# Block means of the second batch by narrow products and transposes, and the last store from another queue

## The chip, the cores and the metric

The kernel runs on one core of a Trainium2 chip. The metric is the device time of one execution in microseconds, the median of several runs; lower is better. TensorE (PE in the profile, PEld for its weight loads) multiplies, VectorE (DVE), ScalarE (ACT) and GpSimd (POOL) do the rest, and SyncE (SP) issues the transfers.

## The reference

Attention over 2 batches, 8 heads, 768 positions and 64 channels, followed by two feed-forward layers on the 1536 tokens:

```
k_sum = k.reshape(B, H, nb, 32, D).max(axis=3)      # nb = 24 blocks of 32 positions
v_sum = v.reshape(B, H, nb, 32, D).mean(axis=3)
scores_l = scale * (q @ k^T), kept where |i - j| < 16
scores_s = scale * (q @ k_sum^T) + log(32)
a = softmax(concat(scores_l, scores_s))
attn = a @ concat(v, v_sum)
x = attn as [1536, 512]
x = ((x @ w_a) * (x @ w_b)) @ w_out                  # width 1536
h = x @ w_in;  out = (h - tanh(h)) @ w_out2          # width 2048
```

What the change touches is `v_sum` of the second batch: 24 means for each of 8 heads and 64 channels, 24 x 512 numbers from 768 x 512.

## The kernel before

The 1536 tokens are three blocks of 512. The first layer runs over blocks and over 12 slices of its width: for each slice a position "a" (x @ w_a, bank "pa"), a position "b" (x @ w_b, bank "pb") and a position "o" (the product added into four banks "acc"). So a block has 36 positions, numbered j = 0, 1, 2 and so on over all blocks. The second layer follows with positions "h" and "o2". Each large product is made of three fp32r products of high and low halves, so that a projection of one slice is 12 matmuls of 512 columns (`proj`, line 374).

The attention of the first eight units of 64 queries is done ahead in an order written out by hand. The other 16 units are planned into the positions of the first layer: `plan(j, fn)` runs a step ahead of position j. A unit goes through T1 (transposes of q, line 269), T2 (scores, line 295, fp32, and softmax), T3 (transposes, line 331) and T4 (product with v, line 344, eight products into two halves of the partitions). In the same positions the weights are decoded (lines 154 to 165) and split in high and low halves (lines 184 and 185) on ScalarE, VectorE and GpSimd.

The order of the instructions on an engine is in part written out and in part found. From position 0 to 71 only SP's order is the program's; on the other engines a planner at build time chooses the order by its own costs and by priorities (the steps T1, T2, T3, T4, W and prep_k get a higher one). From position 72 on all engines follow the program's order. Each engine then works through its list in that order, and waits when an operand isn't ready.

The second batch's means are one step, `mean_v`, planned at position VM + NC + 4 = 13. Before it six transfers load v of that batch in chunks of 128 positions with all eight heads (`load_vch`), two chunks each in the tiles x20a and x20b and two in buffers of the tag "w", which has 36 buffers. The step multiplies each chunk with a slice of a constant, `mavg` [128, 44], that holds 1/32 where a position belongs to a block, and adds all six into one bank "pt" of 24 x 512. ScalarE copies it to a buffer of "w", and `load_vm` copies that by transfers behind the 96 rows of v in the tiles of units 12 to 14. The bank "pt" is also used by T1 and T3 and by half of prep_k.

The results of the last block are four banks of 128 rows. ScalarE copies the first and the third, VectorE the second and the fourth, and SP issues a store of 256 KB behind each copy (line 477).

Of the kernel before, what the change touches and what calls it, by code (L numbers as in the profile page):

```python
# [15 lines left out]
AF = mybir.ActivationFunctionType  # L16
# [23 lines left out]
def band_attention_moe_kernel(ctx: ExitStack, tc: tile.TileContext, q, k, v, w_a, w_b, w_out, w_in, w_out2, out):  # L40
    nc = tc.nc
    mm = nc.tensor.matmul
# [4 lines left out]
    NB = S // BLK  # L47
    NP = H // 2
    KC = DM // 128
    F1 = w_a.shape[1] // 128  # L50
    F2 = w_in.shape[1] // 128
    TB = 512
    NBLK = NT // TB
    NC = S // 128
# [8 lines left out]
    def st(shape, tag, bufs=1, dt=F32):  # L63
        return sb.tile(shape, dt, tag=tag, bufs=bufs, name=tag)

    def pt(tag, shape=(128, 512)):
        return ps.tile(list(shape), F32, tag=tag, name=tag)


    ident = st([128, 128], "ident")  # L70
# [3 lines left out]
    mavg = st([128, 2 * NB - 4], "mavg")  # L74
# [134 lines left out]
    def where(u):  # L209
        b, w = divmod(u, S // 64)  # L210
        return b, w, min(max(w * 64 - WIN, 0), S - KW)
# [18 lines left out]
    vch = {}  # L230
# [4 lines left out]


    def mean_v(tag):
        pp = pt(tag)[0:NB]
        for c in range(NC):
            mm(  # L240
                pp, mavg[:, NB - 4 - 4 * c : 2 * NB - 4 - 4 * c], vch.pop(c).rearrange("p h d -> p (h d)"),
                start=(c == 0), stop=(c == NC - 1),
            )
        vmo[1] = st([NB, H, D], "w", 3 * F1)
        nc.scalar.activation(vmo[1].rearrange("n h d -> n (h d)"), pp, AF.Copy)

# [201 lines left out]
    def late_hi_lo():  # L448
        if late:
            hi_lo(*late.pop())  # L450

    def pos_o2(G, s):
        blk, f = divmod(G, F2)
        if G == N2 - 1:
            late_hi_lo()
        gh, gl = gs.pop(1000 + G)
        if f == 0:
            acc[10 + blk] = [pt(f"acc{d}") for d in range(4)]
        a = acc[10 + blk]
        for c in range(4):  # L460
            cs = slice(c * 128, (c + 1) * 128)
            for n, (g, i) in enumerate(((gh, 0), (gh, 1), (gl, 0))):
                mm(a[c], g[:, cs], s[:, i, :], start=(f == 0 and n == 0), stop=(f == F2 - 1 and n == 2))  # L463
        if f == F2 - 1:
            if blk < NBLK - 1:
                t = [st([128, 2, DM], f"x2{blk}{i}") for i in "ab"]
                o = [t[c // 2][:, c % 2, :] for c in range(4)]
            else:
                t = st([128, 4, DM], "kt")
                o = [t[:, c, :] for c in range(4)]  # L470
            for c in range(4):
                if c % 2:
                    nc.vector.tensor_copy(o[c], a[c])
                else:
                    nc.scalar.activation(o[c], a[c], AF.Copy)
                r0 = blk * TB + c * 128
                nc.sync.dma_start(out[r0 : r0 + 128, :], o[c])


    HALF, WARM, VM, PK, KS = 0, 3, 3, -3, 2  # L480
# [24 lines left out]
    for G in range(N2 + LAG):  # L505
        if G < N2:
            pos.append((pos_h, G, 3 * F1 + 2 * (G % F2)))
        if G == 0:
            pos.append((pos_o, groups[-1], 3 * F1 - 1))
        if G >= LAG:  # L510
            pos.append((pos_o2, G - LAG, 3 * F1 + 2 * ((G - LAG) % F2) + 1))
# [39 lines left out]
    for c in range(NC):  # L551
        plan(VM + c, lambda c=c: load_vch(c, vt2[c // 2][:, c % 2] if c < 4 else st([128, H, D], "w", 3 * F1)))
    plan(VM + NC + 4, mean_v, "pt")
    OFF = -2
    for n, u in enumerate(range(8, 24)):
        j = (n - 8) * 4 + begin[1] + OFF if n >= 8 else n * (begin[1] // 8) + OFF
        b, w, _ = where(u)
# [280 lines left out]
```

## Time and profile before

| what | us |
|---|---|
| median of 3 runs | 666.63 (666.58 to 667.04) |
| profiled execution, whole | 668.39 |
| its span, first to last instruction | 666.6 |
| TensorE busy | 645.6 (97%) |
| VectorE busy | 509.3 (76%) |
| ScalarE busy | 471.9 (71%) |

The runs are without the profiler; the profiled execution is one more. Busy shares are averages over the span and say nothing of single stages. TensorE's matmuls overlap: the duration of one is longer than its distance to the next, so a pitch is read from the time of many. The granted clock is a share of full speed, 2.4 GHz.

### The profile page before, as it was taken

The page shows a single profiled execution, that of the slowest core. Times are in us where ns is not written, and L with a number is a line of the kernel's source. Part 1 is how long each engine was busy: PE and PEld are TensorE (multiplying, and loading weights), DVE is VectorE, ACT ScalarE, POOL GpSimd, SP SyncE. Part 2 cuts the span into 40 slices and gives each one's busy share as a digit, 9 for nine tenths or more (in the row PEclk, how much of TensorE's full clock was granted, in tenths as well). Part 3 has the DMA queues.
Part 4 walks back from the last instruction along what each step waited for, and adds up shares of the span by engine and source line. Part 5 has one row for each costly group of instructions (what it writes and reads, how often), then busy time and mean ns, then how long its engine had stood idle before and what let it go on. Part 6 is the DMA issues. An engine that isn't in the chain of part 4 may idle for free.

```text
span 666.6 us, 9629 instructions
## 1 busy us (share of the span) xinstructions
PE 645.6 (97%) x3240; PEld 520.3 (78%) x3240; DVE 509.3 (76%) x1019; ACT 471.9 (71%) x1002; POOL 208.1 (31%) x223
## 2 busy tenths in 40 slices
PE   7869999999899999999999999999999999999997
PEld 5658776888688888888888888888888888888885
DVE  5899998999766678637877748777777777777775
ACT  3878888788776778645655548777777777777774
POOL 5771122122001111000111134454444454444441
PEclk8989999999999999999999999999999999999999
DMA  9996996464415435413444200000010000010001
GB/s 205 246 204 202 214 225 184 152 187 132 129 55 168 151 107 167 131 48 111 142 143 142 80 1 0 1 0 1 0 64 1 0 1 0 24 40 1 1 0 63
DMA packets 84781, 62.11 MB, mean 93 GB/s; under 512 B 51892, under 2 KB 75444, under 8 KB 84732
## 3 DMA queue, kind: packets, MB, share of 16 engines
q1 hardware_dynamic: 84732, 61.50, 33.3%
q8 instruction: 25, 0.41, 0.2%
q14 instruction: 24, 0.20, 0.1%
HBM read 54.00 MB, written 7.34 MB: 92 GB/s over the span
## 4 chain that ended last, share of the span: by engine, by line
PE 84%; DVE 7%; ACT 3%; DMA 3%; issue 1%; SPq 1%; POOL 0%; DVEq 0%; ACTq 0%
PE acc L463 20%; PE pa L374 18%; PE pb L374 17%; PE acc L402 13%; PE pt L374 5%; PE ps L374 5%; PE ps L295 2%; PE ps L344 1%; PE pt L331 1%; DVE w L164 1%; PE pt L240 1%; DVE w L165 1%; DMA x20a<-in_q_dram 1%; SPq L614 1%; DMA w<-in_k_dram 1%
## 5 line engine op out<-in xcount | busy, mean ns | idle before, releaser
L185 POOL TENSOR_TENSOR wsp<-w,wsp 128x512 fp32r<-128x512 f32 x97 | 127.4, 1332 | 143.8 <-ACT wsp L184 143.8
L184 ACT ACTIVATE wsp<-w 128x512 fp32r<-128x512 f32 x201 | 121.3, 622 | 19.8 <-PE acc L402 10.1
L185 DVE TENSOR_TENSOR wsp<-w,wsp 128x512 fp32r<-128x512 f32 x104 | 74.7, 719 | 41.7 <-ACT wsp L184 41.5
L179 POOL TENSOR_SCALAR w<-w 128x512 f32<-128x512 f32 x52 | 39.5, 763 | 192.8 <-ACT w L154 184.0
L402 PE MATMUL acc<-gh,wsp 128*128 128x512 f32 x288 | 98.1, 400 | 0.0
L374 PE MATMUL pa<-XA,wsp 128*128 128x512 f32 x336 | 84.9, 399 | 4.6 <-DVE XA L726 4.6
L374 PE MATMUL pb<-XA,wsp 128*128 128x512 f32 x336 | 83.8, 395 | 0.9 <-ACT wsp L768 0.5
L463 PE MATMUL acc<-wsp,gh 128*128 128x512 f32 x256 | 80.5, 396 | 0.0
L374 PEld LDWEIGHTS pa<-XA,wsp 128*128 128x128 f32 x336 | 64.0, 191 | 18.7 <-ACT x21a L155 4.7
L374 PEld LDWEIGHTS pb<-XA,wsp 128*128 128x128 f32 x336 | 62.4, 189 | 15.2 <-ACT wsp L768 1.0
L367 ACT ACTIVATE gh<-tg 128x512 fp32r<-128x512 f32 x68 | 42.3, 622 | 30.6 <-DVE tg L390 30.2
L374 PE MATMUL pa<-XB,wsp 128*128 128x512 f32 x240 | 62.0, 402 | 1.4 <-ACT XB L351 1.4
L402 PEld LDWEIGHTS acc<-gh,wsp 128*128 128x128 f32 x288 | 53.4, 188 | 11.8
L374 PE MATMUL pb<-XB,wsp 128*128 128x512 f32 x240 | 60.0, 394 | 0.0
L402 PE MATMUL acc<-gl,wsp 128*128 128x512 f32 x144 | 56.9, 398 | 0.1
L463 PEld LDWEIGHTS acc<-wsp,gh 128*128 128x128 f32 x256 | 48.2, 188 | 11.1
L368 DVE TENSOR_TENSOR gl<-tg,gh 128x512 fp32r<-128x512 f32 x68 | 47.0, 691 | 9.4 <-ACT gh L367 9.3
L374 PEld LDWEIGHTS pa<-XB,wsp 128*128 128x128 f32 x240 | 45.2, 192 | 11.1 <-ACT XB L351 1.6
L374 PEld LDWEIGHTS pb<-XB,wsp 128*128 128x128 f32 x240 | 44.6, 188 | 9.7
L463 PE MATMUL acc<-wsp,gl 128*128 128x512 f32 x128 | 50.4, 394 | 0.0
L463 PE MATMUL acc<-wsp,vw 128*128 128x512 f32 x192 | 46.5, 390 | 0.0
L463 PEld LDWEIGHTS acc<-wsp,vw 128*128 128x128 f32 x192 | 35.9, 188 | 8.1 <-DVE vw L368 0.4
(305 smaller groups left out, 1184.0 us busy)
## 6 DMA issues: line engine op xcount, KB each, us to landing
stage<-in_moe_w_out_dram SPq DMA_DIRECT2D x19, 512.0 KB, 3.4
stage<-in_moe_w_in_dram SPq DMA_DIRECT2D x16, 512.0 KB, 5.2
stage<-in_moe_w_a_dram SPq DMA_DIRECT2D x8, 512.0 KB, 4.5
w<-wsc SPq DMA_DIRECT2D x16, 256.0 KB, 3.5
vw<-in_v_dram SPq DMA_DIRECT2D x19, 192.0 KB, 3.0
stage<-in_moe_w_b_dram SPq DMA_DIRECT2D x7, 512.0 KB, 5.0
wsc<-x21a SPq DMA_DIRECT2D x8, 256.0 KB, 4.8
wsc<-x21b SPq DMA_DIRECT2D x8, 256.0 KB, 5.9
```

The costliest lines, as they stand in the source:

```text
L164: nc.vector.scalar_tensor_tensor(r, t[:, :, 1], -0x40000000, r, op0=ALU.bitwise_and, op1=ALU.bitwise_or)
L165: nc.vector.tensor_tensor(r, r, t[:, :, 0], op=ALU.add)
L179: nc.gpsimd.tensor_scalar(rf, rf, HI_HI, HI_LO, op0=ALU.min, op1=ALU.max)
L184: nc.scalar.activation(s[:, 0, :], r, AF.Copy)
L185: eng.tensor_tensor(s[:, 1, :], r, s[:, 0, :].bitcast(F32), op=ALU.subtract)
L240: mm(pp, mavg[:, NB - 4 - 4 * c : 2 * NB - 4 - 4 * c], vch.pop(c).rearrange("p h d -> p (h d)"), start=(c == 0), stop=(c == NC - 1),)
L295: mm(pp[:, p, 0:NK], qt[:, p, :], kw[:, p, :], start=True, stop=True)
L367: nc.scalar.activation(dst[0], src, AF.Copy)
L368: eng.tensor_tensor(dst[1], src, dst[0].bitcast(F32), op=ALU.subtract)
L374: mm(dst, w, xx, start=(kk == 0 and n == 0), stop=(kk == KC - 1 and n == 2))
L402: mm(acc[blk][d][:, c0:c1], w, t, start=(f == 0 and c0 == 0 and n == 0), stop=(f == F1 - 1 and n == 2))
L463: mm(a[c], g[:, cs], s[:, i, :], start=(f == 0 and n == 0), stop=(f == F2 - 1 and n == 2))
```

## The change

The means of the second batch are computed the other way round. Instead of six products with the constant as weights and 512 columns of v streamed, there are 24 products, one for each chunk and pair of heads, with 128 columns of v (two heads of 64) as weights and 4 columns of the constant streamed; each writes its own 4 columns of a bank as [128 channels of a pair, pair, block]. ScalarE copies these 128 x 96 numbers to a new buffer of "w". Four transposes turn them into 24 x 512 in "pt" again, and the copy to the second buffer is as it was. Nothing is added up over chunks any more, since a block lies in one chunk.

The last of the twelve stores of results (block 2, rows 384 to 511) is issued from ScalarE's queue, the others from SP's as they were.

```diff
     def mean_v(tag):
+        pp = pt(tag)[:, 0 : NP * NB].rearrange("x (p n) -> x p n", p=NP)
+        for c in range(NC):
+            t = vch.pop(c)
+            for p in range(NP):
+                mm(pp[:, p, 4 * c : 4 * c + 4], t[:, 2 * p : 2 * p + 2, :], mavg[:, NB - 4 : NB], start=True, stop=True)
+        vt = st([128, NP, NB], "w", 3 * F1)
+        nc.scalar.activation(vt, pp, AF.Copy)
         pp = pt(tag)[0:NB]
-        for c in range(NC):
-            mm(
-                pp, mavg[:, NB - 4 - 4 * c : 2 * NB - 4 - 4 * c], vch.pop(c).rearrange("p h d -> p (h d)"),
-                start=(c == 0), stop=(c == NC - 1),
-            )
+        for p in range(NP):
+            nc.tensor.transpose(pp[:, p * 128 : (p + 1) * 128], vt[:, p, :], ident)
         vmo[1] = st([NB, H, D], "w", 3 * F1)
         nc.scalar.activation(vmo[1].rearrange("n h d -> n (h d)"), pp, AF.Copy)
...
                 r0 = blk * TB + c * 128
-                nc.sync.dma_start(out[r0 : r0 + 128, :], o[c])
+                (nc.scalar if blk == NBLK - 1 and c == 3 else nc.sync).dma_start(out[r0 : r0 + 128, :], o[c])
```

## Rows read from the trace of the kernel before

**Rows 1.** The page, busy time of each engine and its share of the span.

```profile
PE 645.6 (97%) x3240; PEld 520.3 (78%) x3240; DVE 509.3 (76%) x1019; ACT 471.9 (71%) x1002; POOL 208.1 (31%) x223
```

**Rows 2.** Stretches: busy time of each engine, granted clock, DMA share, GB/s.

```profile
core 0: us, PE busy (x) PEld busy (x) DVE busy (x) ACT busy (x) POOL busy (x), PEclk, DMA share, GB/s
...
106.00:160.00 54.00, 54.00 (x309) 44.19 (x310) 50.20 (x113) 44.07 (x104) 12.67 (x16) 1.00 0.49 150
160.00:176.00 16.00, 15.89 (x88) 12.14 (x87) 14.47 (x35) 13.44 (x35) 2.25 (x3) 1.00 0.47 146
...
285.00:661.00 376.00, 376.00 (x1638) 307.11 (x1637) 275.42 (x421) 256.83 (x453) 139.32 (x113) 1.00 0.10 36
```

**Rows 3.** The chain of waits, 95 to 125 us: start, us, piece, instructions.

```profile
99.79 0.88 PE ps L295 x8
100.67 5.26 PE pt L240 x12
105.93 2.96 PE pb L374 x12
108.90 0.23 PE acc L402
109.13 0.61 PE ps L344 x16
...
119.29 0.44 PE pt L331 x4
119.72 0.89 PE ps L295 x8
```

**Rows 4.** VectorE's timeline behind the step; in brackets the wait and its releaser.

```profile
106.51 0.17 DVE L322 RECIPROCAL sm<-sm 128x4 f32<-128x4 f32 x1
108.93 0.69 DVE L390 TENSOR_TENSOR tg<-pb,ta 128x512 f32<-128x512 f32 x1 [2.26 <-PE pb L374]
```

**Rows 5.** The step of line 240: ns min/median/max, first and last start, shape.

```profile
L240 PEld LDWEIGHTS pt<-x20a,mavg x4: 99/102/103, 100.6 to 101.5; 128*24 128x24 f32 x4
L240 PE MATMUL pt<-x20a,mavg x4: 592/592/610, 100.6 to 101.9; 128*24 128x512 f32 x4
```

**Rows 6.** Groups of weight loads by shape: busy us, mean ns of one, idle before.

```profile
L295 PEld LDWEIGHTS ps<-kw,qbd 128*128 128x128 f32 x96 | 12.6, 195 | 1.4 <-DVE XB L352 0.9
...
L344 PEld LDWEIGHTS ps<-at,vw 120*64 120x64 f32 x256 | 8.8, 137 | 5.4 <-issue 3.4 <-DVE w L161 1.1 <-DVE sm L321 0.4
...
L240 PEld LDWEIGHTS pt<-x20b,mavg 128*24 128x24 f32 x4 | 0.4, 103 | 1.3 <-issue 1.3
```

**Rows 7.** ScalarE's timeline around the step's copy.

```profile
106.05 0.57 ACT L245 ACTIVATE w<-pt 24x512 f32<-24x512 f32 x1
106.53 0.65 ACT L154 ACTIVATE w<-x21b 128x512 f32<-128x512 f32 x1
107.08 1.20 ACT L154 ACTIVATE w<-stage 128x512 f32<-128x512 f32 x2
```

**Rows 8.** Groups on ScalarE, 85 to 180 us: busy us, mean ns.

```profile
L351 ACT ACTIVATE XB<-ps 128x256 fp32r<-128x256 f32 x7 | 2.6, 368 | 0.0
```

**Rows 9.** Timeline of weight loads behind the step.

```profile
109.06 0.55 PEld L344 LDWEIGHTS ps<-at,vw 120*64 120x64 f32 x16 [0.36 <-issue]
109.67 0.20 PEld L269 LDWEIGHTS pt<-ident,w 128*128 128x128 f32 x2
```

**Rows 10.** Stretches around two changes of the granted clock (columns as in rows 2).

```profile
39.30:43.58 4.28, 0.21 (x7) 0.07 (x3) 4.28 (x11) 3.81 (x8) 4.20 (x6) 1.00 0.45 133
43.58:50.41 6.83, 5.86 (x15) 4.21 (x16) 6.62 (x13) 3.45 (x7) 3.03 (x3) 0.50 1.16 217
...
176.70:180.11 3.41, 1.54 (x15) 0.97 (x12) 1.81 (x3) 1.59 (x4) 0.00 (x0) 1.00 0.66 131
180.11:183.53 3.42, 3.42 (x12) 2.84 (x12) 1.52 (x11) 1.62 (x8) 0.00 (x0) 0.50 0.97 303
```

**Rows 11.** All stores of results: issue on SP, ns, first and last start; landing.

```profile
L477 SPq DMA_DIRECT2D out_dram<-kt x4: 332/332/332, 661.3 to 663.5; - x4
...
DMA to landing us min/median/max: 2.0/2.0/2.5
```

**Rows 12.** Timeline of the last copies.

```profile
661.33 2.50 SPq L477 DMA_DIRECT2D out_dram<-kt  x4
...
662.10 0.60 ACT L475 ACTIVATE kt<-acc 128x512 f32<-128x512 f32 x1 [0.79 <-PE acc L463]
662.78 0.69 DVE L473 COPY kt<-acc 128x512 f32<-128x512 f32 x1 [0.68 <-PE acc L463]
```

**Rows 13.** TensorE's timeline at the second fall of the clock.

```profile
179.52 1.55 PE L295 MATMUL ps<-kw,qbd 128*128 128x120 f32 x8 [0.44 <-DVE XB L352]
```

**Rows 14.** What weight loads waited for, 106 to 176 us: total, times, longest.

```profile
PEld pt L331 <- ACT e L324: 0.9, 4, 0.4
PEld pb L374 <- ACT wsp L184: 0.8, 1, 0.8
```

## The prediction

> **What bounds the kernel now.** I read the page's busy times first: TensorE is busy for 97% of the span, VectorE for 76%, ScalarE for 71% [rows 1]. An average hides stages, so the next view is the table of stretches around the edit: between 106 and 160 us TensorE is busy for all of 54.00 us, between 160 and 176 for 15.89 of 16.00, and from 285 to 661 us without a gap [rows 2]. The chain of waits says the same in order of time: from 100 to 125 us each piece is a TensorE piece [rows 3]. VectorE is close behind (50.20 of 54.00 us), but right behind the step that is changed it is VectorE that waits for TensorE, 2.26 us at 108.93 us [rows 4]. So a microsecond that TensorE gains or loses in this step should reach the end nearly whole. The one larger rest of TensorE behind it, 176.70 to 180.11 us with 1.54 us of work [rows 10], is a dependency of the attention on block 1, which moves along with TensorE.
>
> **The products.** Today the step is six fp32 products that show as 12 weight loads of 24 columns and 12 matmuls of 512 columns [rows 5]; in the chain they take 5.26 us, 0.44 us each [rows 3]. In the change each of 24 products has 128 columns of v as weights and streams 4 columns. The products of scores (line 295) show how one splits: four of them are 8 loads and 8 matmuls, so 24 give 48 loads and 48 matmuls. What is the price of one? A load's duration grows with its columns: 103 ns for 24, 137 for 64, 195 for 128 [rows 6], about 0.9 ns a column over a fixed part. Line 295, with loads of 128 columns over matmuls of 120, advances by 0.89 / 8 = 0.111 us a pair [rows 3]; there the load (about 0.9 x 128 = 115 ns by that slope) is as long as the pitch, so the load is what is paid, and a matmul of 4 columns instead of 120 saves nothing. I take 48 x 0.111 = 5.33 us against 5.26: +0.1 us. The bounds: downwards, line 344, whose 64-column loads advance by 0.61 / 16 = 0.038 us [rows 3], 0.076 for 128 columns, 3.66 us in all (-1.6 us); upwards, loads that don't overlap at all with the matmul before them, 48 x 0.195 = 9.36 us (+4.1 us). Line 295 is the nearest row: same type, same 128 columns.
>
> The Trainium skill's page "TensorE: Matmul & The Clock Gate" (section "LDWEIGHTS (loading the stationary operand)") speaks against the change too: a load takes its column count divided by 1.2, in ns, whatever the matmul streams. By it 48 loads are an estimated 5.12 us, a wash with the 5.26 us removed; the trace agrees with 0.111 us for 128 columns, where the rule says 0.107.
>
> **The four transposes.** They move 128 columns of the identity each, over 24 columns of data. The nearest row is line 331, 0.44 us for four [rows 3]: +0.44 us. Below, nothing (no reason allows it); above, 0.6 us if the last one's drain shows.
>
> **The two copies on ScalarE.** The old copy of 24x512 took 0.57 us [rows 7] and stays. A copy of 128x96 comes in; the nearest rows are the 128x256 copies of line 351, 0.37 us [rows 8], so 0.2 to 0.37 us on an engine that has 10 us free in 54 [rows 2]. The transposes wait for it. Behind them on TensorE stands the next projection, 12 matmuls in 2.96 us [rows 3]; the order there is the planner's choice, not written out, and a planner that sees the transposes not ready puts the projection ahead, which covers the copy. If it doesn't, TensorE stands for the copy, and for what ScalarE does first: after the old step three decode steps of 0.65 and 1.20 us lay in its queue [rows 7], so 0.4 to 2.2 us. I take 0. The bank "pt" is held from the first product to the second copy, some 1 us longer; the query transposes of line 269, which use it at 109.67 us [rows 9], wait for it, and after them the scores of the next units; TensorE has projections to do meanwhile. One more buffer of the 36 of "w" is used and soon free: 0.
>
> **The last store.** The four stores are issued from 661.33 us on, one behind each copy, each taking 0.33 us of SP, the last at 663.5 us [rows 11]; VectorE's last copy begins at 662.78 us and takes 0.69 us [rows 12], so it ends at 663.47 and SP is already waiting for it. ScalarE, idle since its copy of 662.10 us, would wait for the same end. Landing takes 2.0 us from either, I take it; no store from ScalarE is in this trace, and the spread of the stores' landings, 2.0 to 2.5 us, bounds it. 0, between 0 and +0.5 us. SP has nothing behind it.
>
> So far 0.1 + 0.44 + 0 + 0 = +0.5 us.
>
> **The clock.** One thing is unlike anything in this stage now. Today the 5.26 us are full of streaming columns. In the change TensorE loads weights for that long and streams 48 x 4 columns. The granted clock in this trace falls to 0.50, which is 1.2 GHz, at 43.58 us, behind a stretch in which TensorE was busy for 0.21 of 4.28 us, and at 180.11 us, behind one with 1.54 us of 3.41; it stayed low for 6.83 and 3.42 us [rows 10]. Neither row says whether weight loads alone keep the clock: in both stretches the loads were few too. I think it likelier than not that they don't, since the array computes next to nothing meanwhile. At the low level everything on TensorE goes at half speed (8 score pairs took 1.55 us around 180 us [rows 13] against 0.89), so a low stretch of 3.42 to 6.83 us loses 1.7 to 3.4 us. I take the middle, 2.6 us; without cover, since TensorE is the bound.
>
> The same page, in its Part 1 (the clock gate), says that the clock follows how busy TensorE has been and, in Part 4, that transposes don't count as busy in the same way; what a load counts for it does not say, and no row here shows it.
>
> **The sum.** +0.5 + 2.6 = +3.1 us, on the profiled span of 666.6 us, 669.7 us. The profiled execution took 668.39 us, 1.8 us more than its span for what lies around it; the runs without profile have their median at 666.63 us, about the span itself, and I add the change to that: 669.7 us.
>
> **Rivals.** (a) The clock holds, because loads count as work. Then +0.5 us, 667.1 us, between 666.6 and 667.9. For it: line 295 loads as much as it streams and never lost the clock by itself. Chance 0.30. (b) The clock holds, but the planner puts the transposes right behind the copy, or the longer use of "pt" holds the attention back: 0.4 to 2.2 us more, in the middle 1.3, 668.4 us. Against it: at no one place from 106 to 176 us do TensorE's loads wait longer than 0.8 us for ScalarE now [rows 14]. Chance 0.12. (c) Faster: the weight loads of narrow products go faster than those of line 295. It decides where a load is paid at less than (5.26 - 0.44) / 48 = 0.100 us; at line 344's 0.076 us for 128 columns the sum is 3.66 + 0.44 - 5.26 = -1.2 us, and with the attention ready earlier for block 1, so that the clock doesn't fall at 180.11 us, 1.7 us more: 663.7 us, and 665.4 us without that. Against it: in line 344 two halves of the array are loaded alternately (h = 0 and 1 write different partitions), here one product takes all 128 columns. Chance 0.13, of which half lies below 665.3 us. The Trainium skill's page "TensorEngine Tiling (Array Packing)", section "Instruction Overhead", would have (c) in a stronger form: a matmul with one column costs as much as one with 60, some 60 cycles, and by it alone 48 of them are an estimated 1.2 us; no run here shows such a row. (d) The store from ScalarE does nothing that can be seen: that is in the sum already.
>
> **Chances and range.** The forecast, clock lost: 0.45, 668.3 to 671. What a measurement of this kernel can tell from no change is about 0.2%, 1.3 us: 665.3 to 668.0. Faster than that: 0.07 of (c) and 0.05 for an order of the planner that falls out better, 0.12. Slower: all 0.45, two thirds of (b), a little of (a), 0.56. The same: 0.32. The range from 666.0 to 671.0 us leaves out (c) and about 0.07 above.
>
> **What would show it.** In the profile after: 48 loads at line 240's successor, advancing by about 0.11 us; the stretch right behind them with a granted clock of 0.50 for 3.4 to 6.8 us, and the projection there at twice its time; four transposes in 0.44 us, not waiting; the last store landing about 2.0 us after 663.5 plus the delay. I am wrong if the granted clock stays at 1.00 there (then 667.1), or if the loads advance by 0.06 us or less, or if TensorE's delay is gone before 285 us because VectorE, and not TensorE, set the pace there.

## The result and the profile after

The changed kernel takes 671.19 us (670.86 to 671.44, 3 runs) against 666.63 us: a ratio of 1.0061, between 1.0044 and 1.0079, so 2.9 to 5.3 us slower. The profiled execution has a span of 669.7 us. Two single executions of the runs below, one of 911 us with the halves and one of 1290 us of the kernel before, were far slower than all others and are left out of the ratios.

The products first, by their line (ns min/median/max, first and last start, shape):

```profile
L242 PEld LDWEIGHTS pt<-mavg,x20a x16: 192/192/192, 100.2 to 101.9; 128*128 128x128 f32 x16
L242 PE MATMUL pt<-mavg,x20a x16: 178/253/253, 100.3 to 101.9; 128*128 128x4 f32 x16
L242 PEld LDWEIGHTS pt<-mavg,x20b x16: 192/290/337, 102.0 to 104.4; 128*128 128x128 f32 x16
...
L242 PEld LDWEIGHTS pt<-mavg,w x16: 289/333/333, 104.6 to 108.9; 128*128 128x128 f32 x16
```

The first 16 loads begin within 1.7 us, 0.11 us apart; one takes 192 ns, as in line 295. In the next 16 the durations reach 337 ns, and most of the last 16 take 333. The stretches (columns as in [rows 2]) say why:

```profile
98.00:100.20 2.20, 2.20 (x15) 1.93 (x14) 2.20 (x6) 1.29 (x4) 0.61 (x1) 1.00 0.34 99
100.20:102.83 2.63, 2.63 (x27) 2.63 (x25) 2.63 (x10) 1.83 (x4) 0.00 (x0) 1.00 0.37 128
102.83:113.07 10.24, 10.24 (x51) 9.33 (x51) 4.73 (x15) 5.62 (x19) 0.00 (x0) 0.50 0.57 172
113.07:116.00 2.93, 2.93 (x14) 2.36 (x14) 1.28 (x2) 1.10 (x2) 0.00 (x0) 1.00 0.00 0
176.00:180.11 4.11, 4.11 (x32) 2.79 (x31) 4.11 (x9) 3.67 (x10) 0.00 (x0) 1.00 0.40 101
180.11:183.53 3.42, 3.10 (x29) 2.71 (x30) 2.68 (x6) 2.04 (x5) 0.00 (x0) 1.00 0.61 169
```

At 102.83 us, 2.6 us into the products, the granted clock falls to 0.50 (1.2 GHz) and stays there for 10.24 us. Until then the weight loads were busy without a gap (2.63 of 2.63 us). VectorE and ScalarE, busy for 2.63 and 1.83 us of the 2.63 us ahead of the fall, work 4.73 and 5.62 us of the 10.24 us in it. In the main they wait for TensorE, VectorE once for 3.95 us:

```profile
114.02 0.69 DVE L394 TENSOR_TENSOR tg<-pb,ta 128x512 f32<-128x512 f32 x1 [3.95 <-PE pb L378]
```

The two last lines of the stretches answer to [rows 10]: where the kernel before rested for 1.87 us and lost the clock at 180.11 us, TensorE rests 0.32 us and the clock holds.

TensorE's timeline behind the products, then the two copies and the last store:

```profile
108.33 1.02 PE L242 MATMUL pt<-mavg,w 128*128 128x4 f32 x4
109.21 4.78 PE L378 MATMUL pb<-XA,wsp 128*128 128x512 f32 x12
...
116.38 0.60 PE L247 MATMUL pt<-ident,w 128*24 128x128 f32 x4
116.74 0.47 PE L406 MATMUL acc<-gh,wsp 128*128 128x512 f32 x1
```

```profile
110.95 0.24 ACT L244 ACTIVATE w<-pt 128x96 f32<-128x96 f32 x1
```

```profile
665.81 0.69 DVE L477 COPY kt<-acc 128x512 f32<-128x512 f32 x1 [0.67 <-PE acc L467]
666.54 0.38 ACTq L481 DMA_DIRECT2D out_dram<-kt  x1
```

The projection that took 2.96 us in the chain before [rows 3], 3.03 us in this view, takes 4.78 us; the clock rises again at 113.07 us, within it. The new copy (0.24 us) lies under it, and the transposes come 5 us later between other products, waiting for nothing. The last store is issued 0.04 us behind VectorE's copy.

### The profile page after: what moved, and what is told of

The parts are those of the page before. It is cut to its first block, busy times and chain, and to the rows that moved or that the text cites. A ratio compares the mean times of both kernels' runs of the same rounds, so it can differ in the third digit from the quotient of the medians.

```text
span 669.7 us, 9702 instructions
## 1 busy us (share of the span) xinstructions
PE 649.2 (97%) x3280; PEld 527.8 (79%) x3280; DVE 507.9 (76%) x1019; ACT 473.5 (71%) x1003; POOL 211.1 (32%) x223
## 4 chain that ended last, share of the span: by engine, by line
PE 81%; DVE 7%; issue 4%; ACT 4%; DMA 2%; SPq 1%; POOL 0%; DVEq 0%; POOLq 0%; ACTq 0%
PE acc L467 20%; PE pa L378 17%; PE pb L378 17%; PE acc L406 13%; PE pt L378 5%; PE ps L378 5%; PE ps L299 2%; PE ps L348 1%; DVE w L164 1%; PE pt L335 1%; SPq L618 1%; DMA x20a<-in_q_dram 1%; DMA x20b<-in_v_dram 1%; ACT e L314 1%; DVE w L161 1%
## 5 line engine op out<-in xcount | busy, mean ns | idle before, releaser
L179 POOL TENSOR_SCALAR w<-w 128x512 f32<-128x512 f32 x52 | 42.3, 819 | 186.7 <-ACT w L154 180.4
L378 PE MATMUL pb<-XA,wsp 128*128 128x512 f32 x336 | 85.9, 402 | 0.5 <-ACT wsp L772 0.5
L378 PE MATMUL pa<-XB,wsp 128*128 128x512 f32 x240 | 59.3, 393 | 0.0
```

The source lines that it names most:

```text
L179: nc.gpsimd.tensor_scalar(rf, rf, HI_HI, HI_LO, op0=ALU.min, op1=ALU.max)
L378: mm(dst, w, xx, start=(kk == 0 and n == 0), stop=(kk == KC - 1 and n == 2))
```

## Experiments

Two theories. The clock theory is the prediction's: the products stream so little that the clock falls. The order theory: the planner's new order, the second copy and the transposes cost it. Ratios are to the kernel before on the same chip.

**Means only.** The whole change with all stores on SP.

```diff
-                (nc.scalar if blk == NBLK - 1 and c == 3 else nc.sync).dma_start(out[r0 : r0 + 128, :], o[c])
+                nc.sync.dma_start(out[r0 : r0 + 128, :], o[c])
```

> The means by narrow products alone; all twelve stores stay on SP's queue. Clock theory (the narrow products stream so little that the granted clock falls to 0.50 behind their first microseconds, and that is what costs): 671.2 us, as the whole change, within 0.5 us, with a stretch of 8 to 11 us at 0.50 from about 103 us on. Store theory (the store from ScalarE's queue costs a part): 0.5 to 1.5 us less than the whole change, 669.7 to 670.7 us.

Measured: 670.49 us, ratio 1.0052 (1.0033 to 1.0071). The low stretch is there with the same length:

```profile
104.90:115.14 10.24, 10.24 (x49) 9.04 (x49) 4.17 (x9) 5.44 (x17) 0.00 (x0) 0.50 0.51 158
```

The means alone cost what the change costs, as far as the intervals tell (2.2 to 4.7 us here, 2.9 to 5.3 us for the whole). By itself this run doesn't part the two theories of its expectation: the median lies in the range of the store theory, 0.2 us below that of the clock theory, and both ranges were worked out for another chip. The next run does.

**Store only.** The kernel before, the last store from ScalarE's queue.

```diff
-                nc.sync.dma_start(out[r0 : r0 + 128, :], o[c])
+                (nc.scalar if blk == NBLK - 1 and c == 3 else nc.sync).dma_start(out[r0 : r0 + 128, :], o[c])
```

> Only the last store goes from ScalarE's queue; the means are as before. The prediction's sum has 0, between 0 and +0.5 us: 666.6 to 667.1 us. Store theory: 667.1 to 668.1 us. No theory here makes it faster than before by more than 0.1 us.

Measured: 667.43 us against 667.43, ratio 1.0001 (0.9989 to 1.0012): nothing that can be seen, and at most 0.8 us. The stores' issues and landings:

```profile
L477 SPq DMA_DIRECT2D out_dram<-kt x3: 332/332/332, 660.0 to 661.4; - x3
...
L477 ACTq DMA_DIRECT2D out_dram<-kt x1: 377/377/377, 662.2 to 662.2; - x1
...
DMA to landing us min/median/max: 2.0/2.0/2.5
```

An issue costs ScalarE 0.377 us where SP takes 0.332. This profile has the order of the kernel before on TensorE, but no fall of the clock near 180 us: its stretch there reads 1.00 with the same rest before it.

```profile
176.30:179.70 3.40, 1.34 (x18) 0.77 (x18) 2.05 (x4) 2.29 (x5) 0.00 (x0) 1.00 0.49 106
179.70:183.10 3.40, 3.29 (x18) 2.88 (x19) 1.34 (x11) 1.63 (x8) 0.00 (x0) 1.00 0.94 269
```

So the fall at 180.11 us in [rows 10] is not in every execution, and this one's span is 665.4 us, 1.2 us below the one shown before.

**Filled to 96 columns.** The whole change; each product streams 92 columns of zeros ahead of its four, which later products overwrite.

```diff
-    mavg = st([128, 2 * NB - 4], "mavg")
+    FW, mavg = 96, st([128, NB + 96], "mavg")
...
-        for c in range(NC):
+        for c in reversed(range(NC)):
...
-                mm(pp[:, p, 4 * c : 4 * c + 4], t[:, 2 * p : 2 * p + 2, :], mavg[:, NB - 4 : NB], start=True, stop=True)
+                mm(pp[:, p, 4 * c : 4 * c + FW], t[:, 2 * p : 2 * p + 2, :], mavg[:, 4 : FW + 4], start=True, stop=True)
```

> The whole change, but each of the 24 products streams 96 columns, 92 of them zeros whose results are overwritten or unused; results as before. The loads stay 48 of 128 columns. Clock theory: the loads advance by 0.111 us as with 4 columns (96 columns at two cycles each, 0.08 us, hide behind a load), the granted clock stays at 1.00 from 100 to 115 us, and the time is 667.1 us, some 4 us below the whole change. Order theory (the loss comes from the other order of the instructions, from the second copy and from the transposes that wait for it): 670 to 671.5 us, since none of that goes away. Load theory (a load costs more than in the rows of line 295): above 671 us or the same.

Measured: 666.71 us against 667.43, ratio 0.9989 (0.9980 to 0.9999), 3.8 us below the means alone on that chip. The stretches of the products and behind them, and the chain:

```profile
99.50:105.60 6.10, 6.10 (x66) 5.94 (x65) 6.10 (x19) 4.87 (x15) 0.00 (x0) 1.00 0.68 218
105.60:116.00 10.40, 10.40 (x50) 8.43 (x50) 4.09 (x8) 7.10 (x17) 2.12 (x4) 1.00 0.32 91
```

```profile
99.78 4.89 PE pt L242 x44
104.68 0.62 PE ps L348 x16
105.29 0.61 PE pt L242 x4
105.91 2.80 PE pb L378 x12
...
112.19 0.44 PE pt L247 x4
```

The clock holds. 44 products in 4.89 us are 0.111 us each: 96 columns cost the same as 4. The 24 products and the four transposes of the change are all here, and the loss is gone. But the planner had put the rest in another order than in the whole change, so two more runs part the two.

**Filled to 40 and to 42 columns.** The same edit with 40, then 42 in place of 96. With 40 the planner's order is that of the whole change on every engine (only the chunks follow each other backwards, as in all filled runs), with 42 that of the run with 96; the streaming of the two is all but the same.

> As the run with 96 columns, with 40 columns streamed in each product; every engine has the same order of instructions as in the whole change. Clock theory: the loads advance by 0.111 us at full clock; the streaming is 40 x 2 cycles, 0.033 us of each 0.111 us. If that is still too little, the clock falls as in the whole change and the time is 671.2 us within 0.7; if it is enough, the clock stays at 1.00 and the time is 667.1 us with the very same order. Order theory: 671.2 us with the clock at 1.00 is what only it would give.

> As the run with 96 columns, with 42 streamed in each product: the streaming is that of the run with 40 columns but for two, while the order of the instructions on every engine is that of the run with 96. So it parts the clock from the order. Clock theory: the clock falls behind the products as with 40 columns, to 0.50 for 6 to 8 us, and the time is 669 to 670.5 us, 2.5 to 3.5 us above the run with 96. Order theory: 666.7 us, the time of the run with 96, whatever the clock does.

Measured: with 40 columns 669.67 us against 667.43, ratio 1.0030 (1.0012 to 1.0047); with 42 columns 668.47 us against 666.98, ratio 1.0018 (1.0004 to 1.0033). The stretches of the two, 40 first:

```profile
100.50:106.14 5.64, 5.64 (x63) 5.54 (x61) 5.64 (x19) 4.57 (x14) 0.00 (x0) 1.00 0.64 205
106.14:112.97 6.83, 6.83 (x22) 5.56 (x19) 2.10 (x5) 3.53 (x10) 0.00 (x0) 0.50 0.48 145
```

```profile
99.50:103.63 4.13, 4.13 (x39) 4.13 (x38) 4.13 (x15) 3.33 (x12) 0.00 (x0) 1.00 0.53 162
103.63:110.46 6.83, 6.83 (x34) 5.77 (x34) 2.71 (x7) 3.44 (x9) 0.00 (x0) 0.50 0.62 183
```

In either order the clock falls, for 6.83 us, and both lose a part of what the whole change loses. With 40 columns the time, 669.67 us, lies between the two that the clock theory allowed (671.2 within 0.7, or 667.1): the low stretch is shorter, and two of the ten runs, of 667.29 and 667.72 us, had a higher mean clock (0.990 and 0.989, the others 0.982 to 0.987). With 42 columns the ten runs of one and the same program lie far apart, and go in part with their mean granted clock over the whole span:

```
mean clock   us
0.992        666.48  666.48
0.991        667.68
0.989        667.82  668.01  669.84  670.72
0.987        668.92  669.15  669.36
```

The two at 0.992 are as fast as the run with 96 columns, with its order; the profiled one (669.36 us), at 0.987, has the fall. The mean is over all of a run, falls elsewhere included, so it doesn't put the rest in order: 670.72 us, the longest, has 0.989. The median came out 0.5 us below the range the clock theory gave; that not all runs lose the clock behind the products is my reading of these means, since only one of the ten has a trace. The order theory, 666.7 us whatever the clock does, falls: with the same order and the same loads the ratio is 1.0018 (from 1.0004) with 42 columns and 0.9989 (to 0.9999) with 96. The order of the whole change with the clock at 1.00 is in no trace; the run of 667.29 us with 40 columns comes nearest to it.

**Halves.** The filled form with 64 columns, each product cut in two of 64 columns of v, into the two halves of the partitions; 60 of the 64 streamed are zeros; stores on SP. The edit is shown against the filled form.

```diff
-                mm(pp[:, p, 4 * c : 4 * c + FW], t[:, 2 * p : 2 * p + 2, :], mavg[:, 4 : FW + 4], start=True, stop=True)
+                for h in range(2):
+                    hs = slice(h * 64, h * 64 + 64)
+                    mm(pp[hs, p, 4 * c : 4 * c + FW], t[:, 2 * p + h, :], mavg[:, 4 : FW + 4], start=True, stop=True)
```

> The change with each product cut in two of 64 columns of v as weights (one head each, into the two halves of the partitions, as line 344 does) and 64 columns streamed, 60 of them zeros; stores on SP. 96 loads of 64 columns. If a load's price goes with its columns and the two halves load at the same time, as in line 344 (0.031 to 0.038 us a load), the products take 3.0 to 3.7 us instead of 5.3 us; if the halves don't help, 5.3 us. Clock theory: the streaming is dense, so the clock stays at 1.00. The time by TensorE alone: 2 us below the run with 96 columns, 664.7 us; since the earlier runs showed slack behind this step, 0.5 to 2 us below it.

Measured: 665.99 us against 667.35, ratio 0.9978 (0.9969 to 0.9987). It beats both kernels, the one before by 0.9 to 2.1 us. The first loads, then the stretches of the products and behind them:

```profile
L244 PEld LDWEIGHTS pt<-mavg,w x32: 132/138/138, 100.1 to 101.0; 128*64 128x64 f32 x32
```

```profile
100.10:103.80 3.70, 3.61 (x113) 3.47 (x112) 3.70 (x14) 2.89 (x10) 0.00 (x0) 1.00 0.56 174
103.80:116.00 12.20, 12.20 (x61) 9.66 (x57) 7.43 (x13) 9.14 (x21) 3.36 (x5) 1.00 0.52 143
```

32 loads begin within 0.9 us, 0.029 us apart, so 96 take 2.8 us where 48 whole ones took 5.3: 0.058 us for 128 columns in two halves against 0.111 in one. The clock holds here too. The products are some 2.5 us shorter than with 96 columns; of that 0.6 us shows at the end by the medians (1.4 us below the kernel before against 0.7), and the two intervals overlap, so what of it reaches the end stays open.

**No products.** The kernel before without the second batch's means; zeros are set instead.

```diff
-        pp = pt(tag)[0:NB]
         for c in range(NC):
-            mm(
-                pp, mavg[:, NB - 4 - 4 * c : 2 * NB - 4 - 4 * c], vch.pop(c).rearrange("p h d -> p (h d)"),
-                start=(c == 0), stop=(c == NC - 1),
-            )
+            vch.pop(c)
         vmo[1] = st([NB, H, D], "w", 3 * F1)
-        nc.scalar.activation(vmo[1].rearrange("n h d -> n (h d)"), pp, AF.Copy)
+        nc.gpsimd.memset(vmo[1], 0.0)
```

> Leaves out the second batch's means: no products and no copy, zeros are set in their place (so the output lacks these means). It asks what TensorE's 5.26 us of this step are worth at the end. If TensorE alone sets the pace: 5.2 us below the kernel before, 661.9 us. If the other engines and the attention's chain set it in part: 1 to 4 us below.

Measured: 662.64 us against 667.35, ratio 0.9941 (0.9925 to 0.9956). By the medians 4.7 of the 5.26 us reach the end, by the interval 2.9 to 5.0 us: most of it. So TensorE's time counts here, as [rows 2, 3] were read.

**Pair sums, and pair sums late.** GpSimd adds neighbouring positions, and three wide products do what six did; in the second run sums and products are planned later.

```diff
+        src = v[1, h0:h1, c * 256 : (c + 1) * 256, :].rearrange("h (t r) d -> t h (r d)", r=2)
...
+    def add_vch(c, h0=0, h1=8):
+        t = vch[c, h0, h1]
+        nc.gpsimd.tensor_tensor(t[:, :, 0:D], t[:, :, 0:D], t[:, :, D : 2 * D], op=ALU.add)
...
+                pp[:, h0 * D : h1 * D], mavp[:, x0 : x0 + NB], vch[c, h0, h1][:, :, 0:D],
+                start=(c == 0), stop=(h0 == 4),
...
-        plan(VM + n + 4, add_vch, c, h0, h1)
+        plan(VM + NC + n, add_vch, c, h0, h1)
```

> The kernel before, with the means of the second batch made from half the rows: GpSimd first adds neighbouring positions (as the first batch's means already do), and three wide products of 512 columns do what six did; all stores on SP. TensorE as the bound: 6 matmuls of 0.43 us go away, 2.6 us less, 664.8 us against 667.4 on that chip; the streams stay wide, so the clock stays at 1.00. Rival (VectorE sets the pace in this stage, or the four sums on GpSimd hold up its other work): 666.5 to 668 us.

> As the run with pair sums, with GpSimd's four sums planned five positions later, when their loads have landed (there they waited 5.6 us for loads, with the clamps of the weights behind them), and the products one position later. If that wait took the gain: 2 us below the kernel before. If not: as before, within 0.7 us.

Measured: 666.58 us against 666.98, ratio 0.9993 (0.9980 to 1.0006), and 666.51 against 667.35, ratio 0.9994 (0.9985 to 1.0004). Neither gains. Both lose ahead of the step a part of the 2.6 us that they save in it; the stretch from 60 to 98 us, pair sums first, then late, then the run with the store only:

```profile
60.00:98.00 38.00, 35.52 (x203) 28.18 (x203) 36.14 (x76) 31.69 (x74) 14.79 (x16) 1.00 0.83 226
```

```profile
60.00:98.00 38.00, 34.98 (x190) 27.26 (x189) 36.02 (x74) 31.32 (x73) 14.22 (x16) 0.96 0.82 224
```

```profile
60.00:98.00 38.00, 37.05 (x213) 30.12 (x212) 36.43 (x78) 31.99 (x74) 8.49 (x12) 1.00 0.92 225
```

TensorE rests 2.5 and 3.0 us there, against 0.95 us. The granted clock of 0.96 in the second line is a fall to 0.50 for 3.41 us at 93.18 us, which this execution (667.97 us, 1.5 us above the median) has besides. That the sums' wait for their loads is the reason was my guess, and planning them later did not cure it; whether the order, the changed loads or the sums themselves hold TensorE up is open. So less work for TensorE in this step makes the kernel faster, as without the products, only where nothing else then holds TensorE up.

## Why the prediction was right, point by point

The forecast, 669.7 us with the clock lost, had the direction and the mechanism; it was 1.5 us short. The measured 671.19 us lies 0.2 us above the upper end of the range that I gave (666.0 to 671.0), which is less than the 1.3 us that I took for what can't be told from no change.

**The clock** was the term that decided, and its mechanism held; its size was short. I took low stretches of 3.42 to 6.83 us from the rows at hand and the middle of what they lose, 2.6 us. The stretch was 10.24 us, which loses half of it, 5.1 us. What I left out: the fall came in the midst of the products and not behind them. By 102.83 us half of them had begun (2.63 / 0.111 = 24 of 48 loads); the others ran at half speed, a load every 0.213 us instead of 0.111, still streaming next to nothing, with only the 16 products of line 348 between them, and the projection behind them. That this made the stretch so long is my reading, not shown by itself: with 40 and 42 columns, where 44 and 42 loads had begun at the fall, it was 6.83 us. Against it stands that the length differs between executions of one order too. The kernel before was low for 6.83 us from 43.58 us on [rows 10], the run with the store only, with the same order, for 10.24 us around the same place:

```profile
41.21:51.45 10.24, 7.68 (x19) 5.65 (x20) 9.63 (x16) 5.66 (x10) 4.61 (x5) 0.50 1.01 238
```

So the rows of one execution did not bound the term, and I took them for bounds. That the low level halves TensorE's speed I read from [rows 13], where the eight pairs began at 179.52 us, 0.59 us before the fall at 180.11; the loads above show it, 0.213 us against 0.111.

**The products**, +0.1 us: right. 0.111 us a load at full clock, with 4, 40, 42 or 96 columns streamed. By the 60 cycles of the Trainium skill's page "TensorEngine Tiling (Array Packing)", section "Instruction Overhead", 48 products would be an estimated 1.2 us; the load of 128 columns hides that, and rival (c) falls for this form. A price below line 344's 0.076 us for 128 columns came where the products are cut in halves, 0.058 us.

**The transposes**, +0.44 us: right, 0.44 us in the chain of the run with 96 columns, and they waited for nothing. **The copies**, 0: right; 0.24 us, where I had 0.2 to 0.37. Rival (b) did not come. **The last store**, 0: right, ratio 1.0001.

**Rival (a)**, the clock holds, is the run with 96 columns: 0.7 us below the kernel before (0.1 to 1.3) where I had 0.5 above. So the sum without the clock was some 1.2 us too high. What gave that back wasn't measured by itself; the order behind the step is another one.

**What reaches the end.** I said that the rest of TensorE before block 1 moves along with it. It didn't stay there: in the kernel before TensorE rested for 1.87 us [rows 10], in the changed one for 0.32 us from 176.00 to 183.53. But most of that rest came up elsewhere. At 128 and 133 us, where TensorE was busy without a gap before [rows 2], it now waits for weights that VectorE and ScalarE split (lines 185 and 184):

```profile
128.91 2.57 PE L378 MATMUL pa<-XA,wsp 128*128 128x512 f32 x10 [0.96 <-DVE wsp L185]
...
133.28 0.50 PE L406 MATMUL acc<-gh,wsp 128*128 128x512 f32 x1 [0.53 <-ACT wsp L184]
```

The stretch from 116 to 200 us in the kernel before, with the store only, and in the changed kernel:

```profile
116.00:200.00 84.00, 82.02 (x464) 66.13 (x463) 72.44 (x175) 65.68 (x164) 12.82 (x17) 0.98 0.43 133
```

```profile
116.00:200.00 84.00, 81.48 (x469) 65.79 (x468) 72.22 (x175) 66.18 (x165) 12.45 (x17) 1.00 0.45 135
```

```profile
116.00:200.00 84.00, 82.20 (x463) 66.56 (x462) 75.17 (x181) 67.70 (x165) 18.35 (x21) 1.00 0.46 136
```

TensorE rests 2.0, 2.5 and 1.8 us. So less rest gives back 0.2 to 0.7 us, too little to explain why of 5.1 + 0.5 = 5.6 us some 4.3 remain in the spans (669.7 against 665.4 us with the store only), and 4.6 in the medians. The run with 96 columns gives a sum that fits: without the fall the change is worth -0.7 us, and -0.7 + 5.1 = 4.4. The same run puts the price of the fall itself at 3.8 us, against the means alone on one chip, though in another order; so it is 3.8 to 5.1 us where I had 2.6. The clock term was too small by 1.2 to 2.5 us and the other terms together too large by 1.2, and the two errors went against each other: that the forecast came within 1.5 us is in part luck.

**The base.** I put the profiled 668.39 us down to what lies around a span. A run without the profiler has that too: the one of 671.19 us has a span of 669.5. What the execution shown before had more than the run with the store only was the fall of the clock at 180.11 us, which by half of its 3.42 us would cost 1.7 us, against 0.5 us more rest in the other from 116 to 200 us; their spans differ by 1.2 us. The median of 666.63 us is of three runs; beside the experiments the same kernel had medians of 666.98 to 667.43 us, so the base itself is uncertain by some 0.8 us.

## What to carry to other kernels

A product with few columns streamed over full weights cost its weight load here, so turning a product round saves nothing until the loads are shorter than the streams that they replace (48 x 0.111 us against 5.26 us); two half-wide loads into the two halves of the partitions cost about half (0.058 us against 0.111). A stretch in which TensorE does little but load weights can cost the clock although its load row shows no gap, and the price falls on the rest of that stretch and on the dense work behind it: look for a granted clock below 1.00 from the edit on, and in more than one execution. Columns of zeros that hide behind a load cost no time, and 96 of them kept the clock in this trace where 40 and 42 did not.

## What was not expected of the hardware

The weight loads were busy for 2.63 of 2.63 us, and the clock fell all the same. The Trainium skill's page "TensorE: Matmul & The Clock Gate", Part 1, says that the clock follows how busy TensorE is; here that wasn't the loads (with 4 columns 0.50 for 10.24 us; with 96 columns behind the same loads 1.00). And one order can have a fall in some executions and not in others: the kernel before has its fall at 180.11 us in one profile, while the run with the store only, with the same order on TensorE, has none there. With 42 columns ten runs of one program gave 666.48 to 670.72 us at mean clocks of 0.992 to 0.987.
